# Two edits to the first batch's opening: the maximum's chain issued ahead of the last values, and three groups of tokens loaded a second time with tokens on partitions

## The chip, the cores and the metric

The kernel runs on one NeuronCore of one Trainium2 chip. The core has a matrix engine (PE, with its weight loads shown as PEld), a vector engine (VectorE, DVE), a scalar engine (ScalarE, ACT), a general engine (GpSimd, POOL) and a queue engine (SyncE, SP) that here only issues DMAs. Each takes its instructions in order; semaphores join them. The metric is the device time of one execution in microseconds (us).

## The reference

An attention through 32 inducing points, for four batches of 12480 tokens of 128 channels, and then a feed-forward layer on all 49920 rows:

```python
def mab(q, kv):
    s = scale * (q @ kv.transpose(0, 2, 1))
    s = s - s.max(-1, keepdims=True)
    a = np.exp(s)
    a /= a.sum(-1, keepdims=True) + 1e-09
    return a @ kv
h = mab(I, x)                 # 32 points attend to all tokens of the batch
y = mab(x, h)                 # every token attends to the 32 results
...
h = y @ w_in                  # 128 x 2048
r = np.maximum(h, 0.0)
g = s * (r * r) + b
return g @ w_out              # 2048 x 128
```

All inputs but the two weights are float32; the weights are float64 (the kernel gets their raw 64-bit words and narrows them to float32 itself).

## The kernel before

**Tiles.** The channels lie on the 128 partitions. A block is 480 tokens (BLK); two blocks are a half-group (SB), four a group (GR). A batch has 26 blocks, 13 half-groups and 7 groups, the last of two blocks. The 2048 hidden columns are 16 tiles of 128, taken two at a time: a pair. A block has eight pairs, the program 832.

**The body.** For each pair (`pair`, line 812) PE makes two products into PSUM (line 823), ScalarE or VectorE takes the ReLU (838, 840), VectorE multiplies it with the positive part again (859, the square), ScalarE squares it once more with rounded output (900), VectorE or GpSimd subtracts for the low part (877), and PE adds the products with w_out to the block's sum (925). The first seven pairs are "native": they take w_out unsplit (`w_out_raw`, a tile called wst in the profile) right after line 859. Beside the pairs of a batch, the attention of the next batch is worked off in small units.

**The opening.** Before the first pair the first batch's inducing points have to be there, and for that all of its tokens. `opening` (line 1011) issues, on SP's queue: x of the seven groups in half-groups with channels on partitions (`load_first`, 373, DMAs of line 381), the four parts of w_in in between (`W_IN_AFTER`), then the four parts of w_out (`load_weight`, 272, DMAs of line 280; they share four buffers called g1, so that a part of w_out waits until w_in's part in that buffer is narrowed, at line 307). Seven groups need seven homes; there are four (`homes`, 355), and groups 4, 5, 6 use again those of 1, 2, 3.

For each group `p1_unit` (413) goes through: scores on PE (432), the group's maximum on VectorE (436, 439), the exponential with its sum on ScalarE (444), its transpose on PE (450) and a copy (eT), the values on PE (461), and a copy of them (tile s). Beside it, for each half-group `turn_x` (398) turns x on PE: eight transposes (407) put tokens on the partitions, 120 at a time, and a copy by ScalarE or VectorE (line 178 or 180, in the helper `copy`) moves them to one of four homes (`home["xn"]`, half-group j in home j mod 4). The values of a group wait for its turned half-groups ("turn", j); after them the home is free ("v done", j). The PSUM of the groups is `banks[g % 4]`: two single banks and the two halves of one tile, `hs[2][:, 0]` and `hs[2][:, 1]`; the turns use `hs[0]` and `hs[1]`.

Since each group used its own maximum, `h_unit` (488) then makes the common one: the maximum over groups (493), a transpose (477), a maximum (480), a scale (483), a product that spreads it (485), a copy (496), the groups' factors (499) and what follows from them (503 to 510, `h_sums` 517). `h_out` (531) sums the groups' values with these factors (539), divides (545) and transposes (547, 550): hT, the inducing points. From hT come the first block's attention (`attend_first`, 739), the product of w_in with it (`w_unit`, 554), which sixteen DMAs (`spread_w`, 577) bring into place, and the first group's attention (`attend`, 693).

**The weights.** `narrow` (288) makes float32 of a part of 512 columns: five operations of VectorE (295, 298, 305, 307, 312) and two of ScalarE (300, 302). `split_w_out` (316) splits w_out for the pairs that are not native.

**The order.** No loop is issued as written. Each unit is a generator that yields its engine, an estimated duration and the events it waits for. `Plan.run` (118) goes through all units on an estimated clock and issues on each engine what comes next by time plus urgency, so the order on each engine is fixed when the program is built; the semaphores between the engines are made from the data. Estimated landing times of DMAs are part of the clock (`landing`, 239: the queue advances by so many us a load). Where a step may run on ScalarE or VectorE, the plan takes the engine that ends first, after a lean has been added (`LEAN`: -0.622 us for ScalarE, which prefers it). Between hT and the first pair PE gets filler products (`keep_warm`, 1043, line 1041). `after` (1050) starts `h_unit`, `h_out` and what follows once all groups' values are copied ("p1", 0, g).

Of the kernel before, what the change touches and what calls it, by code (L numbers as in the profile page):

```python
# [19 lines left out]
P = 128  # L20
T = 120
# [13 lines left out]
WEIGHT = 0.0272  # L35
LEAN = {"ACT": -0.622}
R_LEAN = {"DVE": -0.222, "ACT": 0.024}

# [19 lines left out]

W_IN_AFTER = (1, 3, 3, 4)
WARM = 6  # L60

# [84 lines left out]
@with_exitstack  # L146
def tile_attn_relu2(ctx: ExitStack, tc: tile.TileContext, xT, xN, indT, w_in, w_out, s_rep, b_rep, outT):
    nc = tc.nc
# [123 lines left out]
    def load_weight(gate, name, c):  # L272
        turn, free = ring("g1", 4)
        yield "SP", 0.05, free, *gate
        sl = slice(c * WC, (c + 1) * WC)
        src, dst = (w_in, w_in_sb) if name == "w_in" else (
            w_out.rearrange("p f d -> p (f d)"), w_out_raw.rearrange("p f d -> p (f d)")
        )
        raw = ew.tile([P, WC, 2], I32, name="g1", bufs=4)
        nc.sync.dma_start(out=raw.rearrange("p n w -> p (n w)"), in_=src[:, sl].bitcast(I32))  # L280
        raws[name, c] = raw, turn
        plan.events["raw", name, c] = landing(1.46)
        plan.spawn(narrow((name, c), dst[:, sl], ("raw", name, c)), W_IN_U if name == "w_in" else W_OUT_U)
        if name == "w_out":
            plan.spawn(split_w_out(c), SPLIT_U)
# [87 lines left out]
    def load_first(g):  # L373
# [5 lines left out]
        for j in range(g * GR // SB, (g * GR + blocks_in(g)) // SB):  # L379
            a = j * SB - g * GR  # L380
            nc.sync.dma_start(
                out=t[:, a:a + SB].rearrange("p q t -> p (q t)"), in_=xT[0, :, j * SB * BLK:(j + 1) * SB * BLK]
            )
            plan.events["x half", j] = landing(1.6)
        plan.events["x", 0, g, 1] = plan.events["x", 0, g, 2] = dma[0]

    def x_used(g, what):

        done = left.setdefault(("x", g), set())
        done.add(what)  # L390
        if len(done) < 1 + -(-blocks_in(g) // SB):
            return
        plan.set(("x done", g))
        n = home["x", g]
        if g == left["x"][n][-1] and n:
            plan.set(("xt", 1) if n == 1 else ("r", n - 2))

    def turn_x(g, h, ps, *waits):
# [9 lines left out]
        x_used(g, h)  # L408
        yield dict(ACT=1.05, DVE=1.15), 0.0
        copy(t.rearrange("p a q c -> p a (q c)"), ps[0:T])  # L410
        plan.set(("turn", j))

    def p1_unit(g, ps, *waits):
# [17 lines left out]
        for q in range(nb):  # L431
# [14 lines left out]
            accum_out=d["l"][0:rows, g:g + 1],  # L446
        )
        yield "PE", 0.45
        for q in range(NQ):
            nc.tensor.transpose(ps[0:T, q * P:q * P + rows], e[0:rows, q * T:(q + 1) * T], ident[0:rows, 0:rows])  # L450
        plan.set(("e", e_turn))
        e_turn, e_free = ring_in_order("eT", 3)
        yield dict(ACT=0.59, DVE=0.68), 0.0, *e_free
        eT = sm.tile([T, NQ, P], F32, name="eT", bufs=3)
# [11 lines left out]
        for j in js:  # L466
            plan.set(("v done", j))
            if j >= NSB - 4 and j % 4 < 2:
                plan.set(("xn", j % 4))
        yield dict(ACT=0.28, DVE=0.3), 0.0  # L470
        copy(d["acc"][0:rows, g, :], ps[0:rows, 0:P])
# [539 lines left out]
    def opening():  # L1011
# [3 lines left out]
        for g in range(NG):  # L1015
# [3 lines left out]
            plan.spawn(p1_work(g), FIRST + 0.1 * g)  # L1019
            for h in range(-(-blocks_in(g) // SB)):  # L1020
                plan.spawn(turn_work(g, h), FIRST + 0.1 * g)
            for c in [c for c, after in enumerate(W_IN_AFTER) if after == g]:
# [20 lines left out]
    def keep_warm(ps, *waits):  # L1043
# [4 lines left out]
        plan.set(("h", 0))  # L1048

    def after():  # L1050
        yield "SP", 0.05, *[("p1", 0, g) for g in range(NG)]
        plan.spawn(h_unit(0, lambda: hs[2][:, 0]), FIRST)
        plan.spawn(h_out(0, lambda: hs[2][:, 1]), FIRST)
        plan.spawn(w_work(), FIRST + W_URGENCY)
# [8 lines left out]
    plan.spawn(warm(WARM, lambda: hs[2][:, 1]), 2 * FIRST)  # L1063
    plan.spawn(opening(), 0.0)
    plan.spawn(after(), 0.0)
    with tc.manual_schedule():
# [37 lines left out]
```

## Time and profile before

| | us |
|---|---|
| median of three runs (1607.75 to 1609.3) | 1608.01 |
| the profiled execution | 1608.36 |
| its span, first to last instruction | 1606.3 |
| PE busy | 1592.8 |
| VectorE busy | 1510.3 |
| ScalarE busy | 1457.1 |
| GpSimd busy | 1501.3 |
| moved by DMA | 130.19 MB |

Times in the profile count from the span's first instruction. PE's matmuls overlap, and the ends of its instructions are modelled, so its busy share says that it did not run dry, not that it was at its peak. "L925" is line 925 of the kernel. A row of the timeline or of a group names engine, line, operation, what it writes and reads, shapes and count; in brackets or behind a bar stands the idle time of the engine before it and what ended it. A row of the view by stretches gives a stretch, its length, then busy time and instructions of PE, PEld, VectorE, ScalarE and GpSimd, the clock granted to PE, the busy share of the 16 DMA engines, and GB/s.

### The profile page before, as it was taken

The numbers are of one execution on the slowest core, as the hardware profiler recorded it, in microseconds if no ns is written. First come the engines' busy times: TensorE is split into PE (matmuls) and PEld (weight loads), VectorE is DVE, ScalarE is ACT, GpSimd is POOL, SyncE is SP. The second block draws the span as 40 slices with busy tenths as digits, with TensorE's granted clock in tenths as the row PEclk, the third lists the DMA queues.
The fourth block names the chain that finished last, engine by engine and source line by source line (L and its number), as shares of the span: only waits on it lengthen the run. The fifth ranks groups of instructions, "written<-read, shape, count | busy, mean of one in ns | idle before, by whom it ended". The sixth has DMA issues, their size and how long they took to land.

```text
span 1606.3 us, 24734 instructions
## 1 busy us (share of the span) xinstructions
PE 1592.8 (99%) x8179; PEld 1294.1 (81%) x8179; DVE 1510.3 (94%) x1636; ACT 1457.1 (91%) x1655; POOL 1501.3 (93%) x678
## 2 busy tenths in 40 slices
PE   9899999999999999999999999999999999999998
PEld 6587888888887788888788787888888888888887
DVE  5999999999999999999999999999999999999997
ACT  7798989988999998998999998998999999999997
POOL 0299999999999999999999999999999999999998
PEclk9999999999999999999999999999999999999999
DMA  7332222312133222231212322322222112112100
GB/s 265 101 105 98 75 86 99 112 50 88 43 100 118 79 88 84 84 117 56 79 59 99 105 80 74 118 80 87 75 59 67 37 51 68 31 50 68 51 30 25
DMA packets 53981, 130.19 MB, mean 81 GB/s; under 512 B 11488, under 2 KB 37984, under 8 KB 53856
## 3 DMA queue, kind: packets, MB, share of 16 engines
q1 hardware_dynamic: 53856, 128.63, 25.1%
q8 instruction: 66, 1.08, 0.3%
q14 instruction: 59, 0.48, 0.1%
HBM read 73.52 MB, written 25.56 MB: 62 GB/s over the span
## 4 chain that ended last, share of the span: by engine, by line
PE 97%; DVE 1%; ACT 1%; issue 0%; DMA 0%; POOL 0%; POOLq 0%; DVEq 0%; ACTq 0%
PE x L925 67%; PE h L823 23%; PE x L701 2%; PE x L651 1%; PE x L613 1%; PE h L407 1%; DVE g L859 0%; DMA xt<-in_xT_dram 0%; PE x L432 0%; PE h L461 0%; PE x L563 0%; PE h L432 0%; PE x L461 0%; ACT g L900 0%; DVE wst L312 0%
## 5 line engine op out<-in xcount | busy, mean ns | idle before, releaser
L877 POOL TENSOR_TENSOR g<-g,g 128x960 fp32r<-128x960 f32 x671 | 1500.1, 2286 | 99.5 <-ACT g L900 87.7
L925 PE MATMUL x<-g,w_hi 128*128 128x480 f32 x3300 | 1079.0, 380 | 0.1
L900 ACT ACTIVATE g<-r 128x960 fp32r<-128x960 f32 (+1 forms) x742 | 795.3, 1097 | 37.7 <-PE x L925 20.6
L859 DVE SCALAR_TENSOR_TENSOR g<-h,r 128x960 f32<-128x960 f32 x678 | 764.5, 1148 | 20.9 <-ACT r L838 10.2
L925 PEld LDWEIGHTS x<-g,w_hi 128*128 128x128 f32 x3300 | 618.0, 188 | 107.4 <-issue 8.2
L838 ACT ACTIVATE r<-h 128x960 f32<-128x960 f32 x616 | 592.3, 969 | 71.9 <-PE h L823 64.9
L925 PE MATMUL x<-g,w_lo 128*128 128x480 f32 x1650 | 627.5, 380 | 0.0
L823 PE MATMUL h<-a2t,wst 128*128 128x480 f32 x1664 | 510.9, 388 | 4.9 <-DVE g L859 3.0
L823 PEld LDWEIGHTS h<-a2t,wst 128*128 128x128 f32 x1664 | 302.0, 188 | 95.8 <-issue 34.1
L925 PEld LDWEIGHTS x<-g,w_lo 128*128 128x128 f32 x1650 | 309.6, 188 | 56.4 <-issue 7.1
L840 DVE TENSOR_SCALAR r<-h 128x960 f32<-128x960 f32 x216 | 248.8, 1153 | 28.5 <-PE h L823 26.0
L877 DVE TENSOR_TENSOR g<-h,g 128x960 fp32r<-128x960 f32 x154 | 177.0, 1150 | 4.7 <-ACT g L900 1.1
L859 DVE SCALAR_TENSOR_TENSOR h<-h,r 128x960 f32<-128x960 f32 x154 | 177.9, 1157 | 3.6 <-ACT r L838 3.0
L933 ACT ACTIVATE ob<-x,bias,s_sb 128x480 f32<-128x480 f32 x104 | 78.3, 753 | 17.4 <-PE x L925 17.3
L701 PE MATMUL x<-xt,hT 128*32 128x480 f32 x208 | 28.3, 578 | 0.0
L732 DVE TENSOR_TENSOR hl<-x,hl 128x480 fp32r<-128x480 f32 (+1 forms) x28 | 18.2, 652 | 5.6 <-ACT hl L178 5.5
L651 PEld LDWEIGHTS x<-xn,eT 128*32 128x32 f32 (+1 forms) x630 | 16.9, 109 | 7.0 <-issue 5.0
L651 PE MATMUL x<-xn,eT 128*32 128x128 f32 (+1 forms) x630 | 22.6, 275 | 0.0
L613 PE MATMUL x<-xt,ind_sb 128*32 128x480 f32 x156 | 21.2, 578 | 0.0
L725 DVE STREAM_TRANSPOSE x<-x 128x480 f32<-128x480 f32 (+1 forms) x28 | 19.5, 697 | 0.9
L716 DVE TENSOR_REDUCE x<-x 128x15 f32<-128x480 f32 (+1 forms) x28 | 18.5, 660 | 1.8 <-ACT x L714 1.0
L723 DVE TENSOR_TENSOR x<-x,l 128x480 f32<-128x480 f32 (+1 forms) x28 | 18.6, 665 | 1.0
(151 smaller groups left out, 374.1 us busy)
## 6 DMA issues: line engine op xcount, KB each, us to landing
xt<-in_xT_dram SPq DMA_DIRECT2D x41, 960.0 KB, 5.1
out_dram<-ob SPq DMA_DIRECT2D x104, 240.0 KB, 2.0
a2t<-hl SPq DMA_DIRECT2D x412, 60.0 KB, 2.0
xn<-in_xN_dram SPq DMA_DIRECT2D x18, 512.0 KB, 3.8
xn<-in_xN_dram SPq DMA_DIRECT2D x18, 448.0 KB, 4.3
xt<-in_xT_dram SPq DMA_DIRECT2D x13, 480.0 KB, 4.6
wst<-hl SPq DMA_DIRECT2D x64, 64.0 KB, 2.0
r<-in_xT_dram SPq DMA_DIRECT2D x7, 480.0 KB, 9.0
```

Source lines behind the costliest of these rows:

```text
L613: nc.tensor.matmul(ps[M * q:M * (q + 1), 0:BLK], ind_sb, xt[:, q], start=True, stop=True)
L651: nc.tensor.matmul(ps[M * c:M * (c + 1), 0:P], eT[0:rows, n], xn_tiles[b, g, half][0][0:rows, n - half * TH], start=n < P // M, stop=n + P ...
L701: nc.tensor.matmul(ps[M * q:M * (q + 1), 0:BLK], hT[:, 0:M], xt[:, q], start=True, stop=True)
L725: nc.vector.transpose(out=s, in_=s)
L823: nc.tensor.matmul(h[:, u, 0:BLK], wst[:, c * P:(c + 1) * P], A, start=True, stop=True)
L838: nc.scalar.activation(out=r, in_=hv, func=AF.Relu)
L840: nc.vector.tensor_scalar(out=r, in0=hv, scalar1=0.0, scalar2=None, op0=ALU.max)
L859: nc.vector.scalar_tensor_tensor(out=g, in0=hv, scalar=0.0, in1=r, op0=ALU.max, op1=ALU.mult)
L877: eng.tensor_tensor(out=g2, in0=g, in1=hi.bitcast(F32), op=ALU.subtract)
L900: nc.scalar.activation(out=q["g1_t"][:, sl, :], in_=q["r_t"][:, sl, :], func=AF.Square)
L925: nc.tensor.matmul(o, w, g, start=first and n == 0, stop=left == 0 and n == len(ops) - 1)
L933: nc.scalar.activation(out=ob, in_=o, func=AF.Identity, bias=bias, scale=s_sb)
```

## The change

First edit: a new unit, `maximum`, starts `h_unit` as soon as the exponentials of all seven groups are issued and group 3's values are copied, and no longer after all values; it works in `hs[2][:, 1]` (group 3's bank), and `h_out`, which still waits for all values, takes `hs[2][:, 0]`.

Second edit: for groups 4, 5 and 6 (`TURNED = 4`) x isn't transposed on PE. A second array `xP` holds those tokens with tokens on partitions, prepared on the host, and `load_turned` loads it by half-groups (120 partitions of 4 KB) straight into the homes of the turned x, each when the half-group four before it has been used. A group's x buffer is then free after its scores alone.

Beside them, constants of the plan: the copies of the opening lose ScalarE's preference (`P_LEAN`), and the estimated landings go from 1.6 to 1.22 us for a half-group and from 1.46 to 1.3 us for a part of the weights. The group's `plan.set(("exp", 0, g))` only names the event.

```diff
--- before.py
+++ after.py
@@ -34,6 +34,7 @@
 SLIP = 0.179
 WEIGHT = 0.0272
 LEAN = {"ACT": -0.622}
+P_LEAN = {"ACT": 0.0}
 R_LEAN = {"DVE": -0.222, "ACT": 0.024}
 
 
@@ -57,6 +58,8 @@
 W_URGENCY = 6.4981
 
 W_IN_AFTER = (1, 3, 3, 4)
+
+TURNED = 4
 WARM = 6
 
 
@@ -144,7 +147,7 @@
 
 
 @with_exitstack
-def tile_attn_relu2(ctx: ExitStack, tc: tile.TileContext, xT, xN, indT, w_in, w_out, s_rep, b_rep, outT):
+def tile_attn_relu2(ctx: ExitStack, tc: tile.TileContext, xT, xN, xP, indT, w_in, w_out, s_rep, b_rep, outT):
     nc = tc.nc
     B, _, N = xT.shape
     M = indT.shape[1]
@@ -279,7 +282,7 @@
         raw = ew.tile([P, WC, 2], I32, name="g1", bufs=4)
         nc.sync.dma_start(out=raw.rearrange("p n w -> p (n w)"), in_=src[:, sl].bitcast(I32))
         raws[name, c] = raw, turn
-        plan.events["raw", name, c] = landing(1.46)
+        plan.events["raw", name, c] = landing(1.3)
         plan.spawn(narrow((name, c), dst[:, sl], ("raw", name, c)), W_IN_U if name == "w_in" else W_OUT_U)
         if name == "w_out":
             plan.spawn(split_w_out(c), SPLIT_U)
@@ -381,20 +384,31 @@
             nc.sync.dma_start(
                 out=t[:, a:a + SB].rearrange("p q t -> p (q t)"), in_=xT[0, :, j * SB * BLK:(j + 1) * SB * BLK]
             )
-            plan.events["x half", j] = landing(1.6)
+            plan.events["x half", j] = landing(1.22)
         plan.events["x", 0, g, 1] = plan.events["x", 0, g, 2] = dma[0]
 
     def x_used(g, what):
 
         done = left.setdefault(("x", g), set())
         done.add(what)
-        if len(done) < 1 + -(-blocks_in(g) // SB):
+        if len(done) < 1 + (-(-blocks_in(g) // SB) if g < TURNED else 0):
             return
         plan.set(("x done", g))
         n = home["x", g]
         if g == left["x"][n][-1] and n:
             plan.set(("xt", 1) if n == 1 else ("r", n - 2))
 
+    def load_turned(g):
+
+        for h in range(-(-blocks_in(g) // SB)):
+            j = g * GR // SB + h
+            yield "SP", 0.05, ("v done", j - 4)
+            n = (j - TURNED * GR // SB) * SB * NQ * P
+            nc.sync.dma_start(
+                out=home["xn"][j % 4].rearrange("p a q c -> p (a q c)"), in_=xP[:, n:n + SB * NQ * P]
+            )
+            plan.events["turn", j] = landing(1.22)
+
     def turn_x(g, h, ps, *waits):
 
         j = g * GR // SB + h
@@ -406,7 +420,7 @@
             for q in range(NQ):
                 nc.tensor.transpose(ps[0:T, a, q * P:(q + 1) * P], xt[:, h * SB + a, q, :], ident)
         x_used(g, h)
-        yield dict(ACT=1.05, DVE=1.15), 0.0
+        yield dict(ACT=1.05, DVE=1.15), P_LEAN
         copy(t.rearrange("p a q c -> p a (q c)"), ps[0:T])
         plan.set(("turn", j))
 
@@ -445,12 +459,13 @@
             out=e[0:rows], in_=ps[0:rows, 0:BLK], func=AF.Exp, bias=nm, scale=scale,
             accum_out=d["l"][0:rows, g:g + 1],
         )
+        plan.set(("exp", 0, g))
         yield "PE", 0.45
         for q in range(NQ):
             nc.tensor.transpose(ps[0:T, q * P:q * P + rows], e[0:rows, q * T:(q + 1) * T], ident[0:rows, 0:rows])
         plan.set(("e", e_turn))
         e_turn, e_free = ring_in_order("eT", 3)
-        yield dict(ACT=0.59, DVE=0.68), 0.0, *e_free
+        yield dict(ACT=0.59, DVE=0.68), P_LEAN, *e_free
         eT = sm.tile([T, NQ, P], F32, name="eT", bufs=3)
         plan.set(("eT", "got", e_turn))
         copy(eT[:, :, 0:rows], ps[0:T].rearrange("p (q i) -> p q i", q=NQ)[:, :, 0:rows])
@@ -467,7 +482,7 @@
             plan.set(("v done", j))
             if j >= NSB - 4 and j % 4 < 2:
                 plan.set(("xn", j % 4))
-        yield dict(ACT=0.28, DVE=0.3), 0.0
+        yield dict(ACT=0.28, DVE=0.3), P_LEAN
         copy(d["acc"][0:rows, g, :], ps[0:rows, 0:P])
         plan.set(("p1", 0, g))
 
@@ -1017,8 +1032,11 @@
             if g == 0:
                 nc.sync.dma_start(out=ind_sb, in_=indT)
             plan.spawn(p1_work(g), FIRST + 0.1 * g)
-            for h in range(-(-blocks_in(g) // SB)):
-                plan.spawn(turn_work(g, h), FIRST + 0.1 * g)
+            if g < TURNED:
+                for h in range(-(-blocks_in(g) // SB)):
+                    plan.spawn(turn_work(g, h), FIRST + 0.1 * g)
+            else:
+                plan.spawn(load_turned(g), FIRST + 0.1 * g)
             for c in [c for c, after in enumerate(W_IN_AFTER) if after == g]:
                 yield from load_weight((), "w_in", c)
         for c in range(F // WC):
@@ -1047,10 +1065,14 @@
         plan.set(("g2", warm_turn))
         plan.set(("h", 0))
 
+    def maximum():
+
+        yield "SP", 0.05, *[("exp", 0, g) for g in range(NG)], ("p1", 0, 3)
+        plan.spawn(h_unit(0, lambda: hs[2][:, 1]), FIRST)
+
     def after():
         yield "SP", 0.05, *[("p1", 0, g) for g in range(NG)]
-        plan.spawn(h_unit(0, lambda: hs[2][:, 0]), FIRST)
-        plan.spawn(h_out(0, lambda: hs[2][:, 1]), FIRST)
+        plan.spawn(h_out(0, lambda: hs[2][:, 0]), FIRST)
         plan.spawn(w_work(), FIRST + W_URGENCY)
         plan.spawn(attend_first(lambda: bank[0]), FIRST)
         plan.spawn(keep_warm(lambda: hs[0][:, 1]), FIRST + 190.0)
@@ -1062,6 +1084,7 @@
         plan.events[name, k] = 0.0
     plan.spawn(warm(WARM, lambda: hs[2][:, 1]), 2 * FIRST)
     plan.spawn(opening(), 0.0)
+    plan.spawn(maximum(), 0.0)
     plan.spawn(after(), 0.0)
     with tc.manual_schedule():
         plan.run()
@@ -1085,6 +1108,9 @@
     arrays = {
         "xT": np.ascontiguousarray(x.transpose(0, 2, 1)),
         "xN": xn,
+        "xP": np.ascontiguousarray(
+            x[0, TURNED * GR * BLK:].reshape(-1, T, C).transpose(1, 0, 2).reshape(T, -1)
+        ),
         "indT": np.ascontiguousarray(inducing.T),
         "w_in": np.ascontiguousarray(moe_w_in).view(np.uint64),
         "w_out": np.ascontiguousarray(moe_w_out.reshape(F // P, P, C).transpose(1, 0, 2)).view(np.uint64),
```

## The prediction

> **What bounds the kernel now.** I read the page's part 4 first, then the chain of waits in its first 66 us, then the two long stretches of the body, and then the opening engine by engine.
>
> ```profile
> PE 97%; DVE 1%; ACT 1%; issue 0%; DMA 0%; POOL 0%; POOLq 0%; DVEq 0%; ACTq 0%
> 400.00:800.00 400.00, 399.95 (x2041) 326.75 (x2041) 381.21 (x409) 366.81 (x413) 392.34 (x176) 1.00 0.27 84
> 800.00:1200.00 400.00, 399.90 (x2044) 325.95 (x2043) 381.47 (x406) 366.39 (x412) 392.51 (x177) 1.00 0.27 85
> ```
>
> The first line is the whole chain; the other two come from the view by stretches (busy us and instructions of PE, PEld, DVE, ACT, POOL, then granted clock, DMA share, GB/s). TensorE is busy all the time from the seventies on, and 400 us of it hold 2041 instructions in one stretch and 2044 in the next, 0.15% apart, although the hand-made order differs from place to place. So the body has a rate of its own; what the change can move is the time at which it starts.
>
> ```profile
> 22.28 1.02 PE h L407 x8
> 25.90 1.89 PE h L407 x16
> 30.16 1.02 PE h L407 x8
> 35.42 1.09 PE h L461 x16
> 36.54 0.26 ACT s L178
> 38.28 0.38 PE h L485 x2
> 40.34 0.60 PE h L539 x14
> 41.92 0.28 DVE hT L550
> 54.11 1.07 DVE g L859
> 55.22 1.17 PE h L823 x2
> 56.38 3.20 PE x L925 x4
> ```
>
> This is the chain of waits in the opening (start, length, what). Up to 33 us it runs almost wholly on PE: scores, transposes of x (L407), transposes of the exponentials, values (L461). From the last values at 35.42 it goes through their copy (36.54), the maximum's chain (L485), the sum over groups (h_out, L539), and hT at 41.92; then over VectorE to the first pair's square at 54.11, and back to PE.
>
> ```profile
> 4.00:20.00 16.00, 15.62 (x171) 11.05 (x171) 4.70 (x10) 10.66 (x18) 0.00 (x0) 1.00 1.02 381
> 20.00:36.00 16.00, 14.73 (x220) 10.32 (x219) 13.42 (x31) 13.82 (x26) 0.00 (x0) 1.00 0.62 216
> 36.00:54.00 18.00, 13.43 (x90) 8.08 (x85) 16.53 (x40) 11.71 (x22) 0.00 (x0) 1.00 0.38 105
> ```
>
> By stage: until 20 us PE (15.62 of 16) and the DMA engines (share 1.02) are full and VectorE is nearly idle (4.70). From 20 to 54 us VectorE is busy 29.95 us of 34, so 4.05 us are idle there. This second bound decides my number: after hT nearly everything that VectorE does (the rest of w_out's narrowing, the first attention) stands ahead of the first square at 54.11.
>
> **The change part by part.**
>
> *Transposes that go.* Groups 4, 5, 6 have five half-groups. Four of their transposes are on the chain: 1.02 + 1.89 + 1.02 = 3.93 us; the fifth is not in it. Their copies out of PSUM were all ScalarE's:
>
> ```profile
> L178 ACT COPY xn<-h 120x1024 f32<-120x1024 f32 x7 | 7.1, 1012 | 6.0 <-PE h L407 5.9
> L178 ACT COPY wst<-h 120x1024 f32<-120x1024 f32 x5 | 5.1, 1013 | 0.9 <-PE h L407 0.9
> ```
>
> Five copies at 1.01 us are 5.06 us of ScalarE, in a stretch in which it is 13.82 us busy of 16. If nothing took their place, the last values would come 3.93 us earlier, at 31.5. Something is late next: the data.
>
> *Loads that come.* Five loads of 120 rows of 4 KB (480 KB each) join SP's queue, each waiting for the values of the half four before it, and the last of them therefore for group 4's values, which need the first two.
>
> ```profile
> 16.00:18.00 2.00, 2.00 (x23) 1.96 (x19) 0.15 (x1) 1.77 (x5) 0.00 (x0) 1.00 1.03 408
> 20.00:22.00 2.00, 1.21 (x35) 0.97 (x34) 1.97 (x7) 1.01 (x1) 0.00 (x0) 1.00 1.03 422
> 24.00:26.00 2.00, 2.00 (x42) 1.04 (x43) 1.89 (x4) 1.95 (x4) 0.00 (x0) 1.00 0.90 286
> 26.00:28.00 2.00, 2.00 (x20) 1.99 (x19) 1.99 (x5) 1.96 (x5) 0.00 (x0) 1.00 0.21 84
> 23.57 14.07 SPq L280 DMA_DIRECT2D g<-in_w_out_dram  x4
> DMA to landing us min/median/max: 3.6/3.9/4.4
> 21.20 1.08 PE L461 MATMUL h<-xn,eT 120*32 120x128 f32 x32 [0.79 <-DVE mx L436]
> ```
>
> The DMA engines are full until about 26.2 us (0.90, then 0.21; the last x half was under way till then) at 408 to 422 GB/s. At 415 GB/s one 480 KB load takes 1.18 us of them, five 5.9 us, and a 512 KB part of w_out 1.26 us. With one or two parts of w_out between them (their issues start at 23.57), the last load lands between 26.2 + 5.9 + 1.3 = 33.4 and 34.6. By the dependence: group 2's values (the last row) end at 22.3, the first two loads land behind the queue at 28.6, or 29.8 with w_out's first part ahead; group 4's values take 1.1; the last load is issued near 30 to 31 and lands, by w_out's 3.6 to 4.4 us from issue to landing, between 33.4 and 35.3. So the last values start between 33.4 and 36, and I take **35.0**, nearest to the second way, against 35.42: of 3.93 us on PE, 0.4 are left. The loads' issues on SP are short, and their wait holds up only w_out's parts behind them; w_out's narrowing fills VectorE but is not needed before hT, which hides a delay of some us.
>
> [...]
>
> *The maximum's chain.* Now it is issued behind all groups' values; what it really waits for is the exponentials and maxima.
>
> ```profile
> 33.22 0.66 ACT L444 ACTIVATE e<-h,nm 64x480 f32<-64x480 f32 x1
> 36.54 0.15 DVE L493 TENSOR_REDUCE m<-mx 128x1 f32<-128x7 f32 x1
> ```
>
> From L493 at 36.54 to h_out at 40.34 it takes 3.8 us. The last exponential starts at 33.22; with PE relieved of four transposes and x's last half there at about 26, it should start near 30, and its scores do not depend on the new loads. So the chain runs from about 30.9 to 34.7, under the wait for the last load. That cover is why I charge it nothing; without it (values ready at 31.5) it would lie open for about 3 us. From the last values' start to h_out remain 1.09 + 0.26 + about 0.15 of hand-overs = 1.5 us in place of 40.34 - 35.42 = 4.92. Gain 3.4 us. Together with 0.4: hT comes **3.8 us** earlier, at 38.1.
>
> *VectorE.*
>
> ```profile
> L298 DVE TENSOR_SCALAR g<-g 128x512 int32<-128x512 int32 x8 | 3.3, 416 | 0.0
> L305 DVE SCALAR_TENSOR_TENSOR w_in_sb<-g,w_in_sb 128x512 f32<-128x512 uint32 x4 | 2.7, 687 | 1.0 <-ACT w_in_sb L302 1.0
> L307 DVE SCALAR_TENSOR_TENSOR g<-g,g 128x512 int32<-128x512 int32 x8 | 5.4, 681 | 0.0
> L312 DVE TENSOR_TENSOR w_in_sb<-w_in_sb,g 128x512 f32<-128x512 f32 x4 | 2.7, 676 | 0.0
> L180 DVE COPY eT<-h 120x512 f32<-120x512 f32 x2 | 1.4, 692 | 3.8 <-PE h L432 3.3 <-PE h L450 0.5
> ```
>
> To pass the 3.8 us on, VectorE has to do its 29.95 us between 20 and 50.2, at 99%. It has 2.05 us to move ahead of 20 (L305, L307 and L312 of w_in's first part, 0.69 + 0.68 + 0.68, which wait for ScalarE; it may now leave copies to VectorE early). Against it stands the new lean: ScalarE loses its preference of 0.622 us for copies, so some more go to VectorE, at 0.69 us for an eT. At the present density (88%) with all of the 2.05 moved the end would be 20 + 27.9/0.88 = 51.7, a gain of 2.3; with one eT more (28.6/0.88 = 32.5) it is 1.5. I take half of the move, 28.95 us in 31.0 us (93%), since ScalarE, which VectorE's narrowing alternates with, is relieved by 5 us: **3.0 us**, bounds 1.5 and 3.8.
>
> *Planned landing times* (1.22 and 1.3 for 1.6 and 1.46) cost no instruction; they only order the work. Full-queue loads do take 1.18 and 1.26, so I count nothing. *Freed homes*: x's buffers are released after the scores alone; the next user of them waits for other things. Nothing.
>
> *The clock after 54 us* I leave as it is:
>
> ```profile
> 51.51 0.67 PE L823 MATMUL h<-a2t,wst 128*128 128x480 f32 x2 [1.42 <-DMA wst<-hl]
> 55.22 1.17 PE L823 MATMUL h<-a2t,wst 128*128 128x480 f32 x2 [3.04 <-DVE g L859]
> 56.18 3.40 PE L925 MATMUL x<-g,wst 128*128 128x480 f32 x4
> 62.92 1.77 PE L925 MATMUL x<-g,wst 128*128 128x480 f32 x4
> 56.00:58.00 2.00, 2.00 (x4) 1.00 (x4) 1.93 (x4) 1.21 (x2) 0.00 (x0) 0.50 0.97 392
> ```
>
> PE waits 1.42 and then 3.04 us, the granted clock falls to 0.50, and four products take 3.40 us that take 1.77 at full clock.
>
> **Sum.** The profiled execution took 1608.36 us (its span 1606.3 and 2.1 around it), 0.35 above the median of the three runs. 1608.36 - 3.0 = 1605.36; against the median 1608.01 - 3.0 = **1605.0 us**. The body adds nothing: by the two stretches 0.15% apart it could move by 2.3 us in 1530 if all of it shifted one way, and I allow 1 us.
>
> **The rivals.**
>
> *A. The chain is not hidden (1607.6).* The maximum's chain works in the second half of a PSUM tile of which group 6 uses the first. The trace shows that halves of this tile wait for each other: group 2's values are released by the reduction of group 3, which reads the other half (the row of 21.20 above).
>
> If the order puts the chain's writes behind group 6's copy, the 3.4 us are lost and 0.4 remain. This is also the case in which the change does not do what it says. Against it: if the wait for the last load is real, the chain is through before.
>
> *B. All of it arrives, and the clock stays up (1602.6).* VectorE gets dense (3.8 us), reaches the first square before PE has idled as long as now, and the four products keep 1.77 us: 1.6 us more. 1608.0 - 5.4. For it: ScalarE's 5 us. Against it: the wait of 3.04 us is for VectorE, which then has more w_out work left behind hT, not less.
> [...]
>
> *C. SP's queue holds the last load back (1610.0, slower).* The parts of w_out wait on SP for a buffer that w_in's narrowing frees:
>
> ```profile
> 36.61 0.68 DVE L307 SCALAR_TENSOR_TENSOR g<-g,g 128x512 int32<-128x512 int32 x1
> SPq L280 <- DVE g L307: 11.0, 3, 4.0
> ```
>
> The fourth is free at 37.3. If the last turned load is queued behind it, it lands at 37.3 + 3.9 + 1.2 = 42.4, the last values come 7.0 us late, hT 7.0 - 3.4 = 3.6 us late. VectorE would have done one more part of w_out by then, which gives back up to 2.9 (2.05 and two operations of 0.42): between +0.7 and +3.6, so I take +2.0, near the middle. It decides from the point at which the load is issued after about 33 us. Against it: the load becomes ready near 31, six us before that part.
>
> **How the numbers follow.** Forecast 0.42, A 0.21, B 0.27, C 0.10. A measurement of this kernel tells about 0.2% (3.2 us) from no change, so faster means under 1604.8 and slower over 1611.2. The forecast spreads by its bounds (1.5 to 3.8, and 1 us of the body) across the first line: 0.15 faster, 0.27 same. A: 0.19 same, 0.02 slower. B: faster. C: 0.04 same, 0.06 slower. Faster 0.42, same 0.50, slower 0.08. The range 1601.6 to 1609.0 takes in A and B with 1 us of the body, and leaves out C and the ends.
>
> **What would show it.** Last L461 at 35.0 (34 to 36), released by a DMA and not by PE; L493 ahead of it; under 2 us from it to h_out; hT near 38; VectorE at 93% or more between 20 and 51; the first L859 near 51; clock 0.50 for some us behind it; 2040 to 2045 instructions of PE in 400 us of the body. I am wrong if the last values come by 32 (the data were not late), if L493 stands behind them, if hT moves but the first L859 does not (VectorE), or if the body's count changes.

## The result, and the profile after

| | before | after |
|---|---|---|
| median of five runs (lowest to highest) | 1608.01 us (1607.75 to 1609.3) | 1616.33 us (1615.67 to 1617.38) |
| the profiled execution | 1608.36 us | 1616.36 us |
| its span | 1606.3 us | 1614.6 us |

The changed kernel is **slower**: 1.0051 times the time before, 95% interval 1.004 to 1.0062, some 8.3 us (1616.33 - 1608.01). The forecast was 1605.0, and the range ended at 1609.0.

The body first. The view by stretches of the changed kernel:

```profile
400.00:800.00 400.00, 399.96 (x2040) 325.65 (x2039) 381.99 (x407) 366.54 (x411) 392.26 (x176) 1.00 0.27 85
800.00:1200.00 400.00, 399.91 (x2044) 325.97 (x2042) 380.76 (x407) 367.15 (x414) 392.43 (x177) 1.00 0.27 85
```

2040 and 2044 instructions of PE, as before. The rows of the block results (ob) in two windows say the same; before, then after (durations in ns, then first and last start):

```profile
L933 ACT ACTIVATE ob<-x,bias,s_sb x3: 734/754/755, 77.3 to 107.6; 128x480 f32<-128x480 f32 x3
L933 ACT ACTIVATE ob<-x,bias,s_sb x2: 751/756/762, 1592.0 to 1602.2; 128x480 f32<-128x480 f32 x2
```

```profile
L948 ACT ACTIVATE ob<-x,bias,s_sb x2: 737/744/751, 85.5 to 101.7; 128x480 f32<-128x480 f32 x2
L948 ACT ACTIVATE ob<-x,bias,s_sb x2: 751/754/758, 1600.2 to 1610.4; 128x480 f32<-128x480 f32 x2
```

The first block ends 8.2 us later (85.5 for 77.3), the last one 8.2 us later too (1610.4 for 1602.2). All of the loss is in the opening. Its chain of waits after (start, length, what):

```profile
26.43 11.08 DMA wst<-in_xP_dram
37.56 1.92 PE x L476 x28
39.48 0.30 PE h L492
39.78 0.62 PE h L465 x4
40.49 0.29 DVE mrow L495
...
42.04 0.17 DVE nmall L511
...
42.25 1.95 PE h L476 x16
...
45.70 1.00 PE h L554 x14
```

Before, this part of the chain was PE's own work. Now it is a load of 11.08 us, then the values that it releases (line 476 is the old 461), and only behind these, on PE, the transposes of the maximum's chain (L492, L465). The last values start at 42.25, not at 35.42. By stages:

```profile
4.00:20.00 16.00, 14.78 (x161) 9.80 (x161) 6.95 (x15) 9.02 (x15) 0.00 (x0) 1.00 1.02 388
20.00:36.00 16.00, 11.24 (x147) 6.69 (x144) 11.37 (x25) 9.35 (x19) 0.00 (x0) 0.89 0.92 271
36.00:54.00 18.00, 15.01 (x99) 10.15 (x96) 8.65 (x29) 6.04 (x16) 0.00 (x0) 0.53 0.36 108
```

PE is busy 3.5 us less between 20 and 36 (11.24 for 14.73), and what it saved became idle time. It runs 73 instructions fewer there, 29 of them transposes (15 for 44; in the whole opening 64 are left from 104). VectorE falls from 29.95 to 11.37 + 8.65 = 20.02 us in the 34 us to 54. Of these 9.9 us it had done 2.25 before 20 us (6.95 for 4.70). The other 7.7 us of work still stand ahead of the first square, which moves from 54.02 to 63.09. The DMA engines are busier than before (0.92 for 0.62 in the second row) and move less for it: 271 GB/s at 0.92, where it was 216 at 0.62. The clock after 36 is 0.53.

SP's queue, by the timeline (start, length, what):

```profile
16.26 2.36 SPq L384 DMA_DIRECT2D r<-in_xT_dram  x2
23.14 0.84 SPq L407 DMA_DIRECT2D xn<-in_xP_dram  x2
24.03 1.35 SPq L384 DMA_DIRECT2D r<-in_xT_dram  x1
25.47 0.38 SPq L283 DMA_DIRECT2D g<-in_w_out_dram  x1
25.96 0.82 SPq L407 DMA_DIRECT2D wst<-in_xP_dram  x2
28.16 0.35 SPq L283 DMA_DIRECT2D g<-in_w_out_dram  x1
32.15 0.32 SPq L407 DMA_DIRECT2D xn<-in_xP_dram  x1
```

its waits (total, times, longest), and the tile view of the second loads:

```profile
SPq L407 <- PE h L476: 4.5, 1, 4.5
```

```profile
DMA to landing us min/median/max: 4.9/9.3/11.1
```

The first two turned loads wait 4.5 us on SP for a home, and x's last half is queued behind them. It is issued at 24.03; before, the last x load of this kind started at 19.4 (tile view of the kernel before: times, then first and last start):

```profile
L381 SPq DMA_DIRECT2D r<-in_xT_dram x7: 328/328/495, 3.5 to 19.4; - x7
```

Meanwhile the DMA engines run dry, and once they have work, they are slow (stretches of 2 us):

```profile
22.00:24.00 2.00, 2.00 (x40) 1.38 (x44) 1.25 (x4) 1.46 (x2) 0.00 (x0) 1.00 0.42 166
...
26.00:28.00 2.00, 1.27 (x12) 0.41 (x4) 1.97 (x5) 1.78 (x5) 0.00 (x0) 1.00 1.02 241
...
30.00:32.00 2.00, 1.42 (x26) 1.32 (x28) 0.00 (x0) 0.00 (x0) 0.00 (x0) 0.55 1.03 379
...
34.00:36.00 2.00, 0.73 (x8) 0.17 (x4) 1.50 (x5) 0.65 (x2) 0.00 (x0) 1.00 1.02 234
```

Share 0.42 at 22 to 24; then full (1.02) at 241 and 234 GB/s, where full meant 408 to 422 before. These rows hold all that was under way, w_out's parts too. The row of 30 us has more, 379, and there the clock is 0.55 and VectorE does nothing. It stands still twice (timeline; in brackets the idle time and what ended it):

```profile
32.62 0.29 DVE L183 COPY s<-x 128x128 f32<-128x128 f32 x1 [3.28 <-PE x L476]
36.64 0.69 DVE L315 TENSOR_TENSOR w_in_sb<-w_in_sb,g 128x512 f32<-128x512 f32 x1
40.49 0.28 DVE L495 TENSOR_REDUCE mrow<-h 1x32 f32<-1x128 f32 x1 [3.16 <-PE h L465]
40.70 0.74 DVE L298 TENSOR_SCALAR g<-g 128x512 int32<-128x512 int32 x2
```

It waits 3.28 us to copy a group's values, which wait for a load; before, all seven of these copies were ScalarE's. Then it waits 3.16 us for the maximum's transpose, with w_out's narrowing (L298) behind that wait in its order.

**One scale for all kernels.** The first square was read in the profiles, beside the time of the profiled execution, and beside it how long VectorE was busy from 0 to 54 us (view by stretches):

| | first square at | profiled time | difference | VectorE busy to 54 us | that and the first square |
|---|---|---|---|---|---|
| before | 54.02 | 1608.36 | 1554.34 | 35.60 | 89.62 |
| e9 | 54.12 | 1608.05 | 1553.93 | 35.44 | 89.56 |
| e7 | 55.51 | 1609.17 | 1553.66 | 36.77 | 92.28 |
| e8 | 58.28 | 1611.71 | 1553.43 | 32.66 | 90.94 |
| e3 | 60.33 | 1613.59 | 1553.26 | 30.73 | 91.06 |
| after | 63.09 | 1616.36 | 1553.27 | 27.92 | 91.01 |
| e4 | 64.91 | 1618.11 | 1553.20 | 26.77 | 91.68 |

Over eleven us the rest of the program stays within 1.2. So each experiment below can be read at that one row, and a microsecond there is about a microsecond of the program. The last column says what sets that row: with the second loads the sum stays within 0.8 us, while the first square moves by 6.6. The first square comes when VectorE has done its share of work, and what VectorE idles ahead of 54 us comes back at the end.

### The profile page after: what moved, and what is told of

It reads as the page before. It is cut to its first block, busy times and chain, and to the rows that moved or that the text cites. A ratio compares the mean times of both kernels' runs of the same rounds, so it can differ in the third digit from the quotient of the medians.

```text
span 1614.6 us, 24639 instructions
## 1 busy us (share of the span) xinstructions
PE 1593.7 (99%) x8130; PEld 1293.0 (80%) x8130; DVE 1511.1 (94%) x1638; ACT 1451.6 (90%) x1648; POOL 1501.4 (93%) x678
## 4 chain that ended last, share of the span: by engine, by line
PE 95%; DMA 2%; DVE 1%; ACT 1%; issue 0%; POOL 0%; POOLq 0%; SPq 0%; DVEq 0%; ACTq 0%
PE x L940 67%; PE h L838 23%; PE x L716 2%; PE x L666 1%; PE x L628 1%; DMA g<-in_w_in_dram 1%; DMA wst<-in_xP_dram 1%; DMA xt<-in_xT_dram 0%; DVE g L874 0%; PE h L476 0%; PE x L578 0%; ACT g L915 0%; DVE wst L315 0%; DVE g L310 0%; POOL g L892 0%
```

## The experiments

Line numbers shift by a few from kernel to kernel. Medians; ratios are against the kernel before, with the 95% interval.

**Which edit?** e1 is the kernel before with the first edit alone; e2 is the changed kernel without it.

```diff
+        plan.set(("exp", 0, g))
...
+    def maximum():
+
+        yield "SP", 0.05, *[("exp", 0, g) for g in range(NG)], ("p1", 0, 3)
+        plan.spawn(h_unit(0, lambda: hs[2][:, 1]), FIRST)
...
-        plan.spawn(h_unit(0, lambda: hs[2][:, 0]), FIRST)
-        plan.spawn(h_out(0, lambda: hs[2][:, 1]), FIRST)
+        plan.spawn(h_out(0, lambda: hs[2][:, 0]), FIRST)
...
+    plan.spawn(maximum(), 0.0)
```

> The kernel before with the first edit alone: the maximum's chain behind the exponentials, no second loads, no new constants of the plan. Theory 1 (the second loads are what costs): the chain hides partly, hT comes 1 to 3 us earlier than 41.9, the time is 1605 to 1607.5. Rival (sharing one PSUM tile makes the chain and group 6 wait for each other, as the values of group 6 wait for the copy at line 511 in the changed kernel): hT within 0.5 us of 41.9 or later, 1607.5 to 1610.

> The changed kernel with the maximum's chain back behind all values; second loads, landing times and leans stay. Theory 1: the last values still start near 42, hT at 48 or later, 1616 to 1620, since the loads are the cause. Rival (the chain's interleaving with group 6 is the cause): last values by 38, 1605 to 1609.

e1: 1608.43 us, 1.0003 (0.9994 to 1.0012). e2: 1616.55 us, 1.0050 (1.0034 to 1.0067). The loss is in the second edit and the constants beside it; the first edit alone does nothing that can be measured. e1's timeline shows two waits that the edit brings. It is of an execution of 1611.12 us, 2.7 above e1's median, so it shows that they are there and not what they cost:

```profile
38.83 0.37 ACT L178 COPY eT<-h 120x256 f32<-120x256 f32 x1 [0.56 <-DVE mrow L481]
```

```profile
40.96 0.16 DVE L497 COPY nmall<-h 128x1 f32<-128x1 f32 x1 [1.49 <-ACT s L178]
```

The copy of the last exponentials waits for the maximum's reduction, and the maximum's copy for that of the last values: neither needs the other's data, but they use the two halves of one PSUM tile. In e9 below, where the chain has a bank of its own, both waits are gone.

**The tile.** e9 is e1 with the chain in a bank of its own, free once group 4 is copied; e12 is the same in the changed kernel.

```diff
-        yield "SP", 0.05, *[("exp", 0, g) for g in range(NG)], ("p1", 0, 3)
-        plan.spawn(h_unit(0, lambda: hs[2][:, 1]), FIRST)
+        yield "SP", 0.05, *[("exp", 0, g) for g in range(NG)], ("p1", 0, 4)
+        plan.spawn(h_unit(0, lambda: bank[0]), FIRST)
```

> The kernel before with the first edit alone, as in e1_max_only, but the maximum's chain works in a PSUM tile of its own, free since group 4's values are copied; the order of all instructions is the same as in e1_max_only. Theory 4 (the shared tile takes the chain's gain: chain and group 6 wait for each other's copies there): from the last values' start to hT 4.0 to 4.6 us in place of 5.2, no wait of the copy eT for line 481, time 0.5 to 2 us under e1_max_only (1608.4), 1606.4 to 1608. Rival (VectorE decides when the first square comes, hT does not): hT earlier but first square and time the same, 1608 to 1609.

> The changed kernel, same order, with only the maximum's chain in a PSUM tile of its own. Theory 4: the last values no longer wait 0.25 us for the copy at line 511, nor the group's copy of eT for line 495; last values to hT 5.0 to 5.5 us in place of 5.9; time 1614.8 to 1616. Rival: no change, 1616 to 1617, as the last load lands at 41.5 and the clock is halved.

e9: 1607.17 us, 0.9997 (0.9988 to 1.0006). hT and the first square on VectorE:

```profile
40.58 0.29 DVE L551 COPY hT<-h 128x128 f32<-128x128 f32 x1
54.12 1.15 DVE L860 SCALAR_TENSOR_TENSOR g<-h,r 128x960 f32<-128x960 f32 x1
```

```profile
20.00:36.00 16.00, 14.93 (x218) 10.40 (x218) 13.48 (x31) 13.39 (x26) 0.00 (x0) 1.00 0.59 214
36.00:54.00 18.00, 12.74 (x93) 8.05 (x87) 16.63 (x40) 12.37 (x23) 0.00 (x0) 0.92 0.36 90
```

hT is 1.3 us earlier than before (41.90), and the first square is not earlier at all (54.02 before): VectorE has 13.48 + 16.63 = 30.11 us of its 34 filled, and what hT gains it cannot pass on. e12: 1615.43 us (1613.41 to 1620.03), 1.0057 (1.0042 to 1.0073), not to be told from the changed kernel. The shared tile itself is small: from the last values' start to hT it is 5.22 us in e1 and 4.84 in e9, 5.92 in the changed kernel and 5.49 in e12, 0.4 us each time.

**The constants alone.** e7 is the kernel before with the new lean and the new landing times (1.22 and 1.3), and nothing else.

> The kernel before with the changed constants alone: leans of the opening's copies and planned landings 1.22 and 1.3, transposes on PE and the maximum's chain as before. Theory (the constants cost nothing by themselves): 1606.5 to 1609. Rival (the shorter planned landings put x's readers and w_in's narrowing too early in the order): 1609.5 to 1612, hT after 42.5.

1609.47 us, 1.0009 (1.0 to 1.0019); hT at 43.97, first square at 55.51. By hT this is the rival, by the time it is at the edge of what can be told. A few numbers that cost no instruction delay the first square by 1.5 us in the profile. VectorE has more to do ahead of it (92.28 in the last column for 89.62): without ScalarE's preference it makes three copies of turned half-groups, at 1.22 us, instead of one, and four copies of a group's values instead of none. Which of the constants costs how much was not separated.

**The rate of the loads.** e3 adds eight rows of zeros to xP, so that each load has 128 rows (the last eight are not used). e4 keeps 120 rows, but lays each load's source out in one piece, so that its rows lie 4 KB apart.

```diff
...
-                out=home["xn"][j % 4].rearrange("p a q c -> p (a q c)"), in_=xP[:, n:n + SB * NQ * P]
+                out=home["xf"][j % 4], in_=xP[:, n:n + SB * NQ * P]
...
```

> The changed kernel, each second load with 128 rows (the last eight are zeros that nothing reads), rows 20 KB apart as before. Theory 1a (120 rows are what slows them): packets of 4 KB back from about 300 to 160 ns, a load takes 1.2 to 1.3 us of the full queue in place of 2.0 to 2.5, the last values start at 35 to 37, hT at 39 to 41, time 1605 to 1609. Rival 1b (the stride of 20 KB in the source) and 1c (any load at that place is slow): packets stay at 250 to 300 ns, 1615 to 1618.

> The changed kernel, 120 rows a load, but the source laid out so that each load reads one unbroken stretch (rows 4 KB apart). Theory 1b (stride): packets back to 160 ns, last values at 35 to 37, 1605 to 1609. Theory 1a (120 rows) and 1c: packets stay at 250 to 300 ns, 1615 to 1618.

e3: 1614.26 us, 1.0036 (1.0024 to 1.0048), more bytes and yet faster; e4: 1616.90 us, 1.0055 (1.0040 to 1.0070). The stride of the source is not the cause. e3 by 2 us:

```profile
34.00:36.00 2.00, 0.85 (x9) 0.20 (x8) 1.50 (x4) 0.59 (x2) 0.00 (x0) 0.82 1.02 416
36.00:38.00 2.00, 1.62 (x33) 1.17 (x33) 1.50 (x5) 0.43 (x3) 0.00 (x0) 1.00 1.07 401
```

416 GB/s where the changed kernel has 234, in the same stretch, with the same engines full. So the rate came back as theory 1a had it. The time did not: the last values were expected at 35 to 37 us and the program at 1605 to 1609. They start at 39.49 (chain of waits):

```profile
39.49 1.95 PE h L477 x16
```

The rate is worth 2.8 us there (42.25 in the changed kernel), and there are 4.5 more to the 35.0 of the prediction.

Is a row count that 16 does not divide what is slow? The page's count of packets, before and after:

```profile
DMA packets 53981, 130.19 MB, mean 81 GB/s; under 512 B 11488, under 2 KB 37984, under 8 KB 53856
```

```profile
DMA packets 54656, 132.65 MB, mean 82 GB/s; under 512 B 11563, under 2 KB 38059, under 8 KB 54531
```

The five loads added 675 packets, 75 of them under 512 B: 5 times 120 rows and 5 times 15 small ones. What the 15 small ones of a load are (the expectations below call them completion writes), and how many of the 16 DMA engines a load used, no view here shows. With 15 of 16 a load would take 7% longer; but the rate was nearly halved (234 for 416 GB/s). f1 cuts each load into 112 rows (16 times 7) and 8, f2 into 60 and 60.

```diff
+            for a, z in ((0, 112), (112, T)):
+                nc.sync.dma_start(
+                    out=home["xn"][j % 4][a:z].rearrange("p a q c -> p (a q c)"), in_=xP[a:z, n:n + SB * NQ * P]
+                )
```

> The changed kernel, each second load as two transfers of 112 and 8 rows. If 120 rows are slow because 16 does not divide them (15 engines): the 112 rows (16 x 7) run at full rate, packets of 4 KB near 160 ns, DMA rate in 34:36 near 400 GB/s, 16 + 8 completion writes a load, time 1613 to 1615 as with 128 rows. If it is that rows are not 8 to an engine: packets stay near 300 ns, 230 to 270 GB/s, 1615 to 1617.

> The changed kernel, each second load as two transfers of 60 rows (15 x 4). If 15 engines are the cause: as slow as 120 rows, packets near 300 ns, 230 to 270 GB/s in 34:36, 15 + 15 completion writes a load, 1615 to 1618. If the place of rows 112 to 119 is the cause: the first 60 are fast and the mean is in between, 300 to 330 GB/s.

f1: 1616.43 us, 1.0052 (1.0032 to 1.0072). f2: 1616.33 us, 1.0052 (1.0036 to 1.0068). f1 from 34 to 36 us:

```profile
34.00:36.00 2.00, 0.27 (x4) 0.17 (x4) 1.43 (x4) 0.37 (x2) 0.00 (x0) 1.00 1.03 279
```

It is slow with 112 rows too, though its loads of 8 rows are in the queue as well. The last pair takes them out: all of its loads have a row count that 16 divides. g1 takes e3's 128 rows in two loads of 64 rows (16 times 4); g2 also cuts each in two, but by columns, so that every DMA writes all 128 partitions.

```diff
+            for a, z in ((0, 64), (64, P)):
+                nc.sync.dma_start(out=home["xf"][j % 4][a:z], in_=xP[a:z, n:n + SB * NQ * P])
...
+            for a, z in ((0, 512), (512, 1024)):
+                nc.sync.dma_start(out=home["xf"][j % 4][:, a:z], in_=xP[:, n + a:n + z])
```

> The kernel with 128-row second loads (1614.26 us, DMA at 401 to 416 GB/s between 34 and 38 us, five landings up to 38.5) with each load cut into rows 0 to 63 and rows 64 to 127. Each has 16 times 4 rows. Theory P (the rate falls when the DMA engines of a load do not write to places of SBUF that are separate, and only all 128 partitions at once keep them separate): every half is as slow as the 60-row halves were, 240 to 300 GB/s while these loads are alone in the queue, last values at 41.5 to 43, time within 1.5 us of the changed kernel's 1616.3. Theory R (a row count that is not a multiple of 16, or that does not fill all 16 DMA engines, is what is slow): 64 rows are 16 times 4, so 390 to 420 GB/s, last values at 39 to 40.5, time within 1 us of 1614.3. [...]

> The control for the run beside it: the same 128-row loads cut into two DMAs as well, but by columns (all 128 rows, 2 KB each). Theory P: all 128 partitions are written at once, so the rate stays at 370 to 420 GB/s, last values at 39 to 40.5, time 1613.5 to 1615.5. If cutting a load in two were itself what costs, both runs would be slow alike: under 300 GB/s and about 1616.

g1: 1617.69 us, 1.0057 (1.0042 to 1.0072). g2: 1613.91 us, 1.0034 (1.0021 to 1.0047). g1, then g2:

```profile
34.00:36.00 2.00, 1.38 (x4) 0.00 (x0) 0.89 (x2) 0.39 (x1) 0.00 (x0) 0.72 1.01 272
36.00:38.00 2.00, 0.41 (x4) 0.17 (x4) 1.97 (x6) 0.75 (x2) 0.00 (x0) 1.00 1.05 260
```

```profile
34.00:36.00 2.00, 1.10 (x6) 0.46 (x6) 1.36 (x4) 0.30 (x2) 0.00 (x0) 0.88 1.04 415
36.00:38.00 2.00, 1.93 (x28) 1.34 (x26) 0.00 (x0) 0.00 (x0) 0.00 (x0) 0.50 1.06 412
```

The same bytes into the same places: the engines move 260 to 272 GB/s when the loads go by halves of the partitions, 412 to 415 when each DMA writes all 128. (w_out's parts are under way in these stretches too, in both kernels.) So what is slow in these runs is neither the cut nor a row count that 16 does not divide, but a DMA that does not write all 128 partitions (0.63 to 0.66 of the rate here). The time follows: g2 is with e3, g1 with the changed kernel. (g2's last values, at 41.07, came later than its expectation had them. In the stretch of 36 to 38 us PE's clock is 0.50 in g2 and 1.00 in e3; that this is why is not shown.) Why such a load is slow is not shown; theory P's reason stays a guess, since no view here shows which partition an engine writes, or how many engines a load uses.

**The planned landing.** e5 is the changed kernel with 2.2 in place of 1.22 for the second loads. The loads themselves are the same; e8 has e5's number and e3's rows.

```diff
-            plan.events["turn", j] = landing(1.22)
+            plan.events["turn", j] = landing(2.2)
```

> The changed kernel, but its plan allows 2.2 us for each second load in place of 1.22, about what they took in the profile; the loads themselves stay as they are (120 rows). Theory 2 (part of the loss is the order, made for loads that land earlier: VectorE's work on w_out stands behind the maximum's chain and waits with it): VectorE is busier than 11.4 and 8.7 us in 20:36 and 36:54, the first square comes 2 to 4 us earlier than 63.1, time 1612 to 1614.5. Rival (the late loads alone set it, the order is no matter): first square at 62 to 64, 1615.5 to 1617.

> 128 rows and 2.2 us planned for each second load, both. If the two causes are separate and add up: 2 us under the 128 rows alone (1614.3), 1610.5 to 1612.5. If the order matters only while the loads are slow: 1614 to 1615. Neither theory lets it beat the kernel before: the last half still lands at 37 to 39 behind the queue.

e5: 1613.09 us, 1.0031 (1.0019 to 1.0043). e8: 1611.09 us, 1.0017 (1.0007 to 1.0026). e5's timeline of VectorE and its last stage:

```profile
49.35 0.29 DVE L565 COPY hT<-h 128x128 f32<-128x128 f32 x1 [0.89 <-PE h L562]
60.68 1.15 DVE L874 SCALAR_TENSOR_TENSOR g<-h,r 128x960 f32<-128x960 f32 x1
```

```profile
36.00:54.00 18.00, 13.03 (x103) 9.23 (x103) 10.55 (x33) 7.35 (x16) 0.00 (x0) 0.72 0.54 133
```

hT comes 1.2 us *later* than in the changed kernel (48.17), and the first square 2.4 us *earlier* (63.09): VectorE is busy 10.55 us there and not 8.65. A plan that believes the load to be late puts less of w_out's narrowing behind what waits for it. In e5 the narrowing (L298) stands ahead of the maximum's reduction (L495), which then waits 0.67 us; in the changed kernel it stood behind it, and the wait was 3.16:

```profile
36.65 0.41 DVE L298 TENSOR_SCALAR g<-g 128x512 int32<-128x512 int32 x1
38.13 0.28 DVE L495 TENSOR_REDUCE mrow<-h 1x32 f32<-1x128 f32 x1 [0.67 <-ACT eT L181]
```

**The clock.** e6 adds nine filler products ahead of the values of groups 4, 5 and 6; f4 is e8 with that filler, e10 is f4 with the own bank.

```diff
+        if g >= TURNED:
+            yield from warm(9, lambda: hs[0][:, 1], ("turn", 6), ("turn", 7))
```

> The changed kernel with nine filler products on PE ahead of the values of each of the groups 4, 5 and 6, which keep PE from idling for more than about 2 us there. Theory 3 (the halved clock between 30 and 52 us is part of the loss): granted clock 1.0 in 36:54 in place of 0.53, hT to first square 12 to 13.5 us in place of 14.9, values to hT about 4 in place of 5.9; time 1612.5 to 1614.5. Rival (PE's clock is hidden behind the loads and VectorE): 1615.5 to 1617 at full clock.

> As e10_all_mended, but with the maximum's chain in the shared PSUM tile again: 128 rows, 2.2 us planned, fillers. If the clock gave most: 1609 to 1609.8, 0.3 to 1 above e10_all_mended (1608.8), clock 0.9 or more in 36:54. If the tile gave most: 1610 to 1611, near the 1611.1 without both.

> The changed kernel with 128 rows a load, 2.2 us planned for each, nine fillers ahead of each late group's values, and the maximum's chain in a PSUM tile of its own. If the causes are separate: about 2 us under 128 rows with planned landings (1611.1), 1608 to 1610, clock 1.0 throughout, last values at 38 to 40. If the late last half still sets everything: 1610 to 1611.5.

e6: 1612.09 us, 1.0028 (1.0016 to 1.0040). Its last stage:

```profile
36.00:54.00 18.00, 14.77 (x131) 9.51 (x131) 12.56 (x34) 8.48 (x20) 0.00 (x0) 1.00 0.45 127
```

The clock is 1.00 in place of 0.53. But the filler also moves the plan's clock and with it the order, so the 4.2 us are not the clock's alone: VectorE is busy 12.56 us there for 8.65. The last values start at 43.35, later than in the changed kernel, and yet the first square is at 57.67, 5.4 us earlier; 33.27 us of VectorE to 54 us and this make 90.94, the sum of the table again. On top of e8's rows and landing times, f4 took 1610.48 us, 1.0015 (1.0005 to 1.0024), 0.6 less than e8, which the intervals cannot tell from nothing, though the clock from 36 to 54 us is 0.91 for 0.62; by its expectation the time is the tile's case and not the clock's. e10 took 1608.83, 1.0007 (0.9998 to 1.0016).

**Only the last group.** e13 has e9's bank, the constants of before, 128 rows, 2.2, and loads group 6 alone (`TURNED = 6`).

> The kernel before's constants, the maximum's chain in a PSUM tile of its own, and a second load for the last group alone (one half, 128 rows, 2.2 us planned). One load of 1.26 us comes behind x in a queue that is no longer full; it should land by 35 to 36. If loads hurt by their number and place in the queue: 1606.5 to 1608.5, about as e9_max_own_bank. If any second load costs: 1609.5 or more.

1607.34 us, 0.9997 (0.9988 to 1.0005). Like e9, not to be told from the kernel before. No version here is faster than the kernel before beyond its interval.

## Why the prediction was wrong

**The step that failed is the landing of the second loads, and the cover for it.** "At 415 GB/s one 480 KB load takes 1.18 us of them", the last one lands "by w_out's 3.6 to 4.4 us from issue to landing", and out of these "I take **35.0**" for the last values: they came at 42.25, and the five loads took 4.9, 9.3 and 11.1 us from issue to landing (shortest, median, longest). Then the cover: "w_out's narrowing fills VectorE but is not needed before hT, which hides a delay of some us". It hid nothing: the last values came 6.8 us later and the first square 9.1. VectorE stood still 3.28 and 3.16 us in the wait, and had done 7.7 us less by 54 us. Three things were wrong.

*The rate.* 415 GB/s was read from loads of 128 rows and carried over to 120. While those were in the queue the engines moved 234 and 241 GB/s, at which 480 KB is about 2 us. The weights' parts between them were held up too: they landed after 7.1 to 11.4 us, where it had been 3.6 to 4.4. Mending it (e3) gave 2.1 us of the 8.3, and 2.8 of the 7.25 by which the last values missed the 35.0.

*The queue.* That "their wait holds up only w_out's parts behind them" was wrong: x's last half stood behind the first two loads as well, 4.6 us later than before (24.0 for 19.4), and the DMA engines idled at 22 to 24 us. That was to be had from the diff: `load_turned` runs over groups 4 to 6 on SP while x's own loads are still to come. In e3, too, this order stands (x's last half issued at 25.18), and 4.5 us of the miss are left. No run issues x's last half ahead of the second loads, so how much of them is the queue's stays open.

*The plan.* Of the planned landings it says "they only order the work", and "so I count nothing". The constants alone cost some 1.5 us by medians (e7; at 1.0 to 1.0019 at the edge of what can be told), among them the lean, which the prediction had priced at one copy of 0.69 us. A landing time that fits the real loads gives 3.2 us back (e5). The order decides which work lies behind a wait: e5 and e6 have their last values later than the changed kernel (44.34 and 43.35) and are faster: VectorE is busy 30.19 and 33.27 us to 54 us there, for 27.92.

**The transposes** went off PE as counted (40 of 104 are gone), but what PE saved became waiting: it is 3.5 us less busy between 20 and 36.

**The maximum's chain** was not hidden. The prediction let it run under the wait for the last load. But the values that wait for the load stand ahead of the chain's transposes in PE's order: L492 runs at 39.48, right behind the values of 37.56. Here the wait on PE covered only what other engines could do without PE. Rival A's mechanism, the shared tile, is real as well (the rows of e1), at 0.4 us. Where no load is in the way (e9), 3.16 us remain between the last values (35.74) and h_out (38.90), against 4.92 before and the 1.5 that were forecast: a gain of 1.8, not 3.4, of which hT keeps 1.3.

**VectorE as the second bound** was right: e9 moved hT and not the first square. Only the direction was missed. A full engine cannot gain, but it can lose: by 54 us it was 7.7 us behind, since its own order put free work behind a late wait, and the first square came 9.1 us later. The 2.05 us that the prediction moved ahead of 20 us did move there (2.25).

**The clock** was expected at 0.50 for some us after 54 us. It fell to 0.55 at 30 us already, with PE waiting for loads (1.96 us ahead of the values of 30.58), was 1.00 again from 34 to 36, and 0.53 from 36 to 54.

**The body** was right: it moved by 8.2 us at both ends.

**Rival C** had the sign and the place: its point of decision was a last load issued after about 33 us, and it was issued at 32.15, a little under it. Its 42.4 for the last values is within 0.2 of the 42.25 measured, by luck: its cause (a home of w_out on SP) was not the one. And its price of 2.0 leaned on VectorE working on meanwhile, which it did not.

**What the 8.3 us are**, by medians, each step on top of the one before: 128 rows 2.1 (e3), the planned landing 3.2 (e8), filler 0.6 (f4), the own bank 1.7 (e10; 0.6 by the first squares of the two profiles, 57.36 and 56.74), rest 0.8. The sum from the changed kernel to e8 is outside both intervals (1.004 to 1.0062 and 1.0007 to 1.0026); no single step is, and another sequence would share them out differently. That of the rate is borne out by more kernels: of those that differ in these loads alone, the five that load by fewer than 128 rows have medians of 1616.33 to 1617.69, the two with 128 rows 1614.26 and 1613.91.

## What to carry to other kernels

Before a transfer is priced by the rate of its neighbours, compare the number of partitions it writes: here, with loads in the queue that left some of the 128 out, the full engines moved about 60% of the rate (from 34 to 36 us 211 to 279 GB/s in five kernels, 415 and 416 in the two with 128 rows), and what stood behind them landed later (w_out's parts after 7.1 to 11.4 us, before 3.6 to 4.4). Before a load is put into a queue with a wait of its own, list what is issued behind it. On an engine that works in order a wait is cover only for the other engines; list what stands behind it in its own queue, and behind the waits that it causes elsewhere. Where a planner issues the work, its estimated times are part of the program: give it the measured landing time with the load.

## What the runs showed that was not expected

With loads that write 64 of 128 partitions at a time the full DMA engines move 260 to 272 GB/s, with loads that write all of them 412 to 415, for the same bytes and destinations. A load padded from 120 to 128 rows moves 7% more bytes and lands sooner (median 7.1 us from issue, not 9.3): 416 GB/s, not 234, in the same two microseconds. The last values and hT do not set the time by themselves: VectorE's idle time ahead of the first square does. And the rest of the program is very stiff: between the first square and the end lie 1553.2 to 1554.3 us in the seven kernels of the table, and 1552.8 to 1554.3 in all nineteen, whatever was done ahead of it.
